# Where the reloads of x and of the last modulation weights are issued, in a conditioned linear-attention and SwiGLU block

## Chip, cores and metric

The kernel runs on one core of one Trainium2 chip. The metric is the device time of one execution in microseconds (us). The engines of a core are named as in the profile: PE (TensorE, matrix products; its weight loads are shown apart as PEld), DVE (VectorE), ACT (ScalarE), POOL (GpSimd) and SP (SyncE, which here issues nearly all DMA transfers).

## What is computed

```python
x = A_x                                            # (1, 2048, 1024), bf16
mod = (silu(c) @ w_mod).reshape(c.shape[0], 6, 1, -1)
sa, ca, ga, sb, cb, gb = (mod[:, i] for i in range(6))

h = layernorm(x) * (1 + ca) + sa
q, k, v = split(h @ wqkv)                          # 32 heads of 32
pq, pk = phi(q), phi(k)                            # phi(t) = (t+1 if t>0 else exp(t)) + 1e-6
kv = einsum('bhsd,bhse->bhde', pk, v)
z = einsum('bhsd->bhd', pk)
o = einsum('bhqd,bhde->bhqe', pq, kv) / (einsum('bhqd,bhd->bhq', pq, z)[..., None] + 1e-6)
x = x + ga * (o @ wo)

h = layernorm(x) * (1 + cb) + sb
x = x + gb * ((silu(h @ w_gate) * (h @ w_up)) @ w_down)     # F = 3584
```

There are 2048 rows of 1024 elements; everything is bf16 in DRAM, and the vector c is a single row.

## The kernel before

The 2048 rows are 16 row tiles of 128 rows (`st` 0 to 15), four of which make a chunk of 512 (`ch` 0 to 3). The kernel is one straight program. Every operation is recorded once through helpers (`P.pe`, `P.dve`, `P.act`, `P.pool`, `P.dma`); each engine runs its operations in the order in which they were recorded, and a recorder derives from the reads and writes of each operation which semaphores it has to wait for. All recorded operations therefore carry the line of one helper, L176, in the profile; a few that are recorded otherwise have their own (L905 for the load of Wo, L955 for `rb`, L1079 for gate and up weights). `P.wait_for(engine, ops)` (L195) puts only a wait into an engine's stream. `P.dma` goes to SP unless another queue is named.

The stages in the order of PE's work:

- *q and k.* The tile `XRES` (16 row tiles of x, 32 KB a partition) is loaded, normalized in place, transposed and scaled, and multiplied with Wq and Wk. After this, `XRES` holds the normalized x and no longer x itself.
- *kv* (`g_group` and `g_evac`, L913 and L920). Sixteen groups `g`, each of 16 matmuls over all row tiles, multiply phi(k) with the normalized x in `XRES`. In the last group, PE reads row tile 0 first and row tile 15 last. Between the groups stand `kvt_mm(half)` (L962), 128 short matmuls with 32 columns that form the 32x32 blocks of kv, and `m_mm(half, nh, banks)` (L972), 16 short matmuls that multiply them with Wo into the tile `MW`; ACT and DVE copy the results of `m_mm` out of PSUM. `scale_pq` (L959) divides phi(q), in `PQT`, by the denominators that stand in `RB`.
- *The Wo stage* (from L1033, in the main from L1083). `wo_part(st, nh, hgs)` (L992) multiplies `PQT` with `MW` for row tile `st` and half `nh` of the columns, eight matmuls of 128x512 into one of four PSUM banks in turn. `wo_res(st, nh)` (L998) is the residual on DVE: it adds the bank to the row tile in `XRES`, which by then has to hold x again, and takes the row's sum with it. The first halves of the products for row tiles 0 and 1 are run earlier, mixed with `kvt_mm(1)` and `m_mm(1, ...)`. The order of the residuals is (0,0), (1,0) in the first turn of the loop, (0,1), (1,1) in the second, and from then on both halves of row tile `st` in turn `st`. Beside it, ACT squares each finished row tile (`ln2_sq`), DVE makes mean and variance after every fourth (`ln2_rstd`), and DVE accumulates `macc(STGX[0], kt)` in turns 1 to 6, eight steps of 1024 columns by which a part of the modulation is formed without PE. Turn 7 normalizes chunk 0 and issues its transposition (`th2_dma`) and the first four pairs of gate and up weights (`gu_load`).
- *The FFN* (from L1107). For each chunk: 28 tiles of F with gate and up products, then the product with W_down, the final residual and the stores. In chunk 0, `macc(STGX[1], ft)` is run for the first eight tiles of F.

The two tiles `STGX[0]` and `STGX[1]` (2 MB each) take parts of `w_mod` and lie where `RB` was; so the load into `STGX[1]` (`stgx2`) may start when `scale_pq` of the last four head groups has read `RB`. The reloads of x write into `XRES` and so wait for the last kv group to have read the row tiles in question: `xr0` to `xr3` one row tile each (256 KB), `xr4`, `xr5` and `xr6` four row tiles each (1 MB, rows 512-1023, 1024-1535 and 1536-2047). The order on SP around the change is: `stgx1` (during group 10), `stgx2`, `xr0` to `xr3`, `xr4` to `xr6`, the transposition of the modulation part (`macc_split`, the tile `mhlt`), `th2_dma`, `gu_load`.

Of the kernel before, what the change touches and what calls it, by code (L numbers as in the profile page):

```python
# [9 lines left out]
ALU = mybir.AluOpType  # L10
# [252 lines left out]
def bass_adaLN_cond__linear_attn_block__swiglu_ffn__prompt_kernel(  # L263
# [16 lines left out]
    NCH = 4  # L280
# [5 lines left out]
    with ExitStack() as es:  # L286
# [6 lines left out]
        def T(name, off, shape, dt):  # L293
            n = 1
            for s_ in shape[1:]:
                n *= s_
            assert off % 32 == 0 and off + n * mybir.dt.size(dt) <= ARENA, (name, off, shape)
            return nc.alloc_sbuf_tensor_at(name, shape, dt, offset=base + off)

        KB = 1024  # L300
        XRES = T("xres", 0, [128, NST, D], BF16)
# [30 lines left out]
        SUMXH = T("sumxh", SM + 2816, [128, NST, 2], FP32)  # L332
# [17 lines left out]
        STGX = [T("stgx%d" % i, (72 + 16 * i) * KB, [128, NDT, D], BF16) for i in range(2)]  # L350
# [28 lines left out]
        PS = nc.alloc_psum_tensor("ps", [128, 8, 512], FP32)  # L379
# [5 lines left out]
        xv = A_x[0].rearrange("(t p) d -> p t d", p=128)  # L385
# [6 lines left out]
        wmv = w_mod.rearrange("(kt p) n -> p kt n", p=128)  # L392
        cv8 = c.rearrange("o (kt p) -> (o kt) p", p=128)

        P = _Prog()
# [223 lines left out]
        for f in s0_:  # L619
# [10 lines left out]
               op0=ALU.mult, op1=ALU.mult)  # L630
# [80 lines left out]
        def macc(src, kt):  # L711
            if kt == 0:
                P.dve("tensor_scalar", out=ACC[:], in0=src[:, kt, :], scalar1=SILUF[:, kt:kt + 1], scalar2=None,
                      op0=ALU.mult)
            else:
                P.dve("scalar_tensor_tensor", out=ACC[:], in0=src[:, kt, :], scalar=SILUF[:, kt:kt + 1], in1=ACC[:],
                      op0=ALU.mult, op1=ALU.add)

        def macc_split():
            P.dve("tensor_copy", out=MHL[:, 0, :], in_=ACC[:])  # L720
            P.dve("tensor_tensor", out=MHL[:, 1, :], in0=ACC[:], in1=MHL[:, 0, :], op=ALU.subtract)
            xbar(MHLT[:], MHL[:].rearrange("p i d -> p (i d)"))

        def mod_red():
            P.dve("tensor_reduce", out=RED[:], in_=MHLT[:].rearrange("d (i m) p -> d m i p", i=2),
                  axis=mybir.AxisListType.XY, op=ALU.add)

        def mod_fin_col(idx, plus_one):
            P.dve("tensor_copy", out=MODTMP[:, 0:8], in_=RED[:])
            if plus_one:  # L730
                P.dve("tensor_scalar", out=MODTMP[:, 0:8], in0=MODTMP[:, 0:8], scalar1=1.0, scalar2=None,
                      op0=ALU.add)
            P.dve("tensor_copy", out=MODCOL[:, idx, :], in_=MODTMP[:, 0:8])
# [186 lines left out]
        def g_evac(g):  # L920
            h, dt = g // NDT, g % NDT
            bank = G_BANKS[1 if g == 14 else g % 5]
            i = g % 2
            P.act("activation", out=GTMP[:, i, :], in_=ZB[:, h * 512:(h + 1) * 512], func=ACT.Copy,
                  scale=MODCOL[:, 1, dt:dt + 1])
            P.dve("scalar_tensor_tensor", out=G[:, dt, h * 512:(h + 1) * 512], in0=PS[:, bank, :],
                  scalar=MODCOL[:, 0, dt:dt + 1], in1=GTMP[:, i, :], op0=ALU.mult, op1=ALU.add)
# [44 lines left out]
        def m_mm(half, nh, banks):  # L972
            for k in range(4):
                for g in range(4):
                    h = (g + k) % 4
                    P.pe("matmul", out=PS[32 * h:32 * h + 32, banks[g], :],
                         lhsT=KVT[32 * g:32 * g + 32, half, 32 * h:32 * h + 32],
                         rhs=WO[32 * g:32 * g + 32, 4 * half + h, nh * 512:(nh + 1) * 512], start=True, stop=True,
                         skip_group_check=True)
            for g in range(4):  # L980
                dst = MW[:, 4 * half + g, nh * 512:(nh + 1) * 512]
                if g % 2 == 0:
                    P.act("activation", out=dst, in_=PS[:, banks[g], :], func=ACT.Copy)
                else:
                    P.dve("tensor_copy", out=dst, in_=PS[:, banks[g], :])
# [6 lines left out]
        def wo_part(st, nh, hgs):  # L992
            bank = WO_BANKS[(2 * st + nh) % 4]
            for hg in hgs:
                P.pe("matmul", out=PS[:, bank, :], lhsT=PQT[:, hg, st * 128:(st + 1) * 128],
                     rhs=MW[:, hg, nh * 512:(nh + 1) * 512], start=(hg == 0), stop=(hg == NHG - 1))

        def wo_res(st, nh):  # L998
            bank = WO_BANKS[(2 * st + nh) % 4]
            xs = XRES[:, st, nh * 512:(nh + 1) * 512]  # L1000
            P.dve("scalar_tensor_tensor", out=xs, in0=PS[:, bank, :], scalar=1.0, in1=xs, op0=ALU.mult,
                  op1=ALU.add, accum_out=SUMXH[:, st, nh:nh + 1])

        ev = 0
        for g in range(16):
# [21 lines left out]
            if g == 10:  # L1027
                P.dma("stgx1", STGX[0][:], wmv[:, :, 3072:4096])
        g_evac(15)
        P.dma("stgx2", STGX[1][:], wmv[:, :, 5120:6144])  # L1030
        for st in range(4):
            P.dma("xr%d" % st, XRES[:, st, :], xv[:, st, :])
        wo_part(0, 0, range(4))  # L1033
# [5 lines left out]
        wo_part(1, 0, range(1, 4))  # L1039
        wo_part(1, 1, range(4))  # L1040
        m_mm(1, 1, [4, 5, 7, 6])
        for ch in range(1, NCH):
            P.dma("xr%d" % (3 + ch), XRES[:, 4 * ch:4 * ch + 4, :], xv[:, 4 * ch:4 * ch + 4, :])

        def ln2_rstd(ch):
            sl = slice(4 * ch, 4 * ch + 4)
# [8 lines left out]
        def ln2_xn(st):  # L1055
            P.dve("tensor_scalar", out=XN2[:, :, st % 4, :], in0=XRES[:, st, :].rearrange("p (dt q) -> p dt q", q=128),
                  scalar1=MEAN2[:, st:st + 1], scalar2=RSTD2[:, st:st + 1], op0=ALU.subtract, op1=ALU.mult)

        def th2_dma():
            xbar(H2T[:].rearrange("p dt (j s) -> p (dt j) s", j=4), XN2[:].rearrange("p dt j q -> p (dt j q)"))  # L1060

        def th2_mod():
            for dt in range(NDT):
                P.pool("tensor_scalar", out=H2T[:, dt, :], in0=H2T[:, dt, :], scalar1=MODCOL[:, 2, dt:dt + 1],
                       scalar2=MODCOL[:, 3, dt:dt + 1], op0=ALU.mult, op1=ALU.add)

        def ln2_sq(st):
            P.act("activation", out=JUNK[:], in_=XRES[:, st, :], func=ACT.Square, accum_out=SUMSQ[:, st:st + 1])
            if st % 4 == 3:
                ln2_rstd(st // 4)  # L1070

        def gu_load(q):
            slot = q % 4
            p = q % 14
            g_out, g_in = GUG[slot][:], wgv[:, :, p * 256:(p + 1) * 256]
            u_out, u_in = GUU[slot][:], wuv[:, :, p * 256:(p + 1) * 256]

            def fn(e):
                return [e.dma_start(out=g_out, in_=g_in), e.dma_start(out=u_out, in_=u_in)]  # L1079

            P.add("sp", fn, reads=[], writes=[g_out, u_out], lane="gu%d" % slot, ninc=2, tag="gu_load")

        for st in range(NST):  # L1083
            for (sw, nh) in (((0, 0), (1, 0)), ((0, 1), (1, 1)))[st] if st < 2 else ((st, 0), (st, 1)):
                wo_part(sw, nh, range(4, 8) if st < 2 else range(8))
                wo_res(sw, nh)
            if st >= 1:
                ln2_sq(st - 1)
            for kt in ((), (0,), (1,), (2, 3), (4,), (5,), (6, 7))[st] if st < 7 else ():
                macc(STGX[0], kt)  # L1090
            if st == 6:
                macc_split()
            if st == 8:
                mod_red()
                mod_fin_col(3, False)
            if st == 7:
                for jj in range(4):
                    ln2_xn(jj)
                th2_dma()
            if st == 8:  # L1100
                th2_mod()
            if st == 7:
                for q in range(4):
                    gu_load(q)
        ln2_sq(NST - 1)
        out_ops = []
        for ch in range(NCH):  # L1107
            nxt = ch + 1 if ch + 1 < NCH else None
            for ft in range(NFT):
# [27 lines left out]
                if nxt is None and ft in (8, 12):  # L1137
# [3 lines left out]
                          in1=GB_B[:, 896:1024].unsqueeze(1).to_broadcast([128, f1 - f0, 128]), op=ALU.mult)  # L1141
# [5 lines left out]
            for j in range(4):  # L1147
                st = 4 * ch + j
# [7 lines left out]
                for nh in range(2):  # L1156
                    i = nh
                    parts = [(0, 384, bb + 1), (384, 512, 4)] if last and nh == 1 else [(0, 512, bb + nh)]
                    for (c0, c1, pb) in parts:
# [5 lines left out]
                        xs = XRES[:, st, nh * 512 + c0:nh * 512 + c1]  # L1165
# [45 lines left out]
```

## Time and profile before

| what | value |
|---|---|
| median of 9 runs | 830.0 us (829.29 to 830.31) |
| profiled execution, its own time | 829.29 us |
| its span in the profile | 827.6 us |
| last kv group's matmuls end, Wo stage's go on | about 186.0 us |
| first gate matmul of the FFN | 244.86 us |
| granted TensorE clock | 1.00 |
| DMA traffic over the whole run | 119.32 MB, mean 144 GB/s |

The span runs from the first to the last instruction that the profiler recorded, and the rest of the execution's time lies around it. Times inside the profile count from the span's start. "Busy" is the time in which an engine executes something; registers, branches, semaphores and the issuing of DMAs don't count. In a timeline row the columns are start, length, engine, line, operation, output tile and input tile, how many instructions were merged, and in brackets the idle time before them and what ended it. In a row of waits they are the waiting engine and tile, who released it, the idle time in total, how often, and the longest. SPq rows are DMA issues, and their length is that of the issuing alone.

### The profile page before, as it was taken

The numbers are of one execution on the slowest core, as the hardware profiler recorded it, in microseconds if no ns is written. First come the engines' busy times: TensorE is split into PE (matmuls) and PEld (weight loads), VectorE is DVE, ScalarE is ACT, GpSimd is POOL, SyncE is SP. The second block draws the span as 40 slices with busy tenths as digits, with TensorE's granted clock in tenths as the row PEclk, the third lists the DMA queues.
The fourth block names the chain that finished last, engine by engine and source line by source line (L and its number), as shares of the span: only waits on it lengthen the run. The fifth ranks groups of instructions, "written<-read, shape, count | busy, mean of one in ns | idle before, by whom it ended". The sixth has DMA issues, their size and how long they took to land.

```text
span 827.6 us, 10508 instructions
## 1 busy us (share of the span) xinstructions
PE 820.8 (99%) x4323; PEld 376.2 (45%) x4323; DVE 311.6 (38%) x664; ACT 197.4 (24%) x336; POOL 40.5 (5%) x59
## 2 busy tenths in 40 slices
PE   8999999999999999999999999999999999999998
PEld 4544444444444444444444444444444444444444
DVE  5797997476945521121221112122111211221111
ACT  4757643123242111011111101111110111111011
POOL 1010000000130000030000003000000300000000
PEclk9999999999999999999999999999999999999999
DMA  9969656866397985700455570045557004553000
GB/s 320 289 151 230 150 160 158 183 183 259 70 260 231 288 255 156 177 27 20 131 152 151 153 178 30 20 127 155 150 152 187 26 17 126 152 152 88 0 26 26
DMA packets 199360, 119.32 MB, mean 144 GB/s; under 512 B 57992, under 2 KB 183056, under 8 KB 199312
## 3 DMA queue, kind: packets, MB, share of 16 engines
q1 hardware_dynamic: 199296, 118.65, 53.1%
q8 instruction: 34, 0.56, 0.3%
q14 instruction: 14, 0.11, 0.0%
q10 hardware_dynamic: 16, 0.00, 0.0%
HBM read 100.67 MB, written 4.33 MB: 127 GB/s over the span
## 4 chain that ended last, share of the span: by engine, by line
PE 99%; DMA 0%; DVE 0%; issue 0%; ACT 0%; SPq 0%
PE ps L176 99%; DMA xres<-in_A_x_dram 0%; DVE stats L176 0%; ACT xres L176 0%; SPq L176 0%; DVE xres L176 0%; DVE mv L176 0%; DVE nmr L176 0%
## 5 line engine op out<-in xcount | busy, mean ns | idle before, releaser
L176 PE MATMUL ps<-h2t,gug 128*128 128x512 bf16 x896 | 211.7, 379 | 0.0
L176 PE MATMUL ps<-h2t,guu 128*128 128x512 bf16 x896 | 211.7, 379 | 0.0
L176 DVE TENSOR_TENSOR at<-sg,ps 128x512 bf16<-128x512 bf16 x112 | 77.0, 687 | 282.8 <-PE ps L176 281.2
L176 ACT ACTIVATE sg<-ps 128x512 bf16<-128x512 f32 x112 | 66.9, 597 | 309.7 <-PE ps L176 309.7
L176 PEld LDWEIGHTS ps<-h2t,guu 128*128 128x128 bf16 x896 | 87.7, 98 | 105.7
L176 PEld LDWEIGHTS ps<-h2t,gug 128*128 128x128 bf16 x896 | 87.6, 98 | 105.5
L176 PE MATMUL ps<-wd_a,at 128*128 128x512 bf16 (+1 forms) x512 | 112.4, 377 | 0.0
L176 PE MATMUL ps<-ht,wqk 128*128 128x512 bf16 x512 | 111.7, 379 | 0.0
L176 PE MATMUL ps<-wd_b,at 128*128 128x512 bf16 (+1 forms) x384 | 85.0, 377 | 0.0
L176 DVE TENSOR_TENSOR ut<-att,gb_b 128x512 bf16<-128x512 bf16 (+1 forms) x32 | 14.7, 458 | 166.5 <-ACT att L176 166.5
L176 PEld LDWEIGHTS ps<-wd_a,at 128*128 128x128 bf16 x512 | 50.1, 98 | 59.7
L176 PEld LDWEIGHTS ps<-ht,wqk 128*128 128x128 bf16 x512 | 49.4, 98 | 58.8 <-DVE ht L176 0.4
L176 ACT ACTIVATE att<-ps 128x512 bf16<-128x512 f32 (+1 forms) x32 | 17.4, 591 | 182.1 <-PE ps L176 182.1
L176 PEld LDWEIGHTS ps<-wd_b,at 128*128 128x128 bf16 x384 | 37.6, 98 | 44.7
L176 PE MATMUL ps<-mw,pqt 128*128 128x512 bf16 x256 | 56.2, 379 | 1.2 <-issue 1.2
L176 PE MATMUL ps<-pk,xres 128*128 128x512 bf16 x256 | 56.2, 379 | 0.0
L176 POOL TENSOR_SCALAR h2t<-h2t,modcol 128x512 bf16<-128x512 bf16 x32 | 26.3, 837 | 383.0 <-DMA h2t<-xn 383.0
L176 ACT ACTIVATE e<-ps 128x512 bf16<-128x512 f32 x56 | 33.1, 603 | 31.7 <-PE ps L176 20.2
L176 PEld LDWEIGHTS ps<-mw,pqt 128*128 128x128 bf16 x256 | 24.7, 98 | 31.5 <-issue 1.9
L176 PEld LDWEIGHTS ps<-pk,xres 128*128 128x128 bf16 x256 | 24.7, 98 | 29.9 <-issue 0.9
L176 ACT ACTIVATE junk<-xres 128x1024 bf16<-128x1024 bf16 x24 | 25.4, 1058 | 35.8 <-DVE xres L176 35.5
L176 DVE SCALAR_TENSOR_TENSOR xres<-ps,xres 128x512 bf16<-128x512 f32 x32 | 21.5, 688 | 13.1 <-PE ps L176 12.9
(107 smaller groups left out, 337.0 us busy)
## 6 DMA issues: line engine op xcount, KB each, us to landing
gug<-in_B_w_gate_dram SPq DMA_DIRECT2D x56, 512.0 KB, 3.9
guu<-in_B_w_up_dram SPq DMA_DIRECT2D x56, 512.0 KB, 5.2
xres<-in_A_x_dram SPq DMA_DIRECT2D x20, 256.0 KB, 7.9
rb<-recip_den SPq DMA_DIRECT2D x8, 512.0 KB, 11.5
stgx<-in_w_mod_dram SPq DMA_DIRECT2D x2, 2048.0 KB, 8.4
wd_a<-in_B_w_down_dram SPq DMA_DIRECT2D x4, 1024.0 KB, 7.3
out_dram<-xres SPq DMA_DIRECT2D x31, 128.0 KB, 1.7
xres<-in_A_x_dram SPq DMA_DIRECT2D x3, 1024.0 KB, 14.1
```

The source lines that it names most:

```text
L176: return getattr(e, method)(**kw)
```

## The change

Two things in the order of SP's program change, and nothing in the order of the other engines.

The load `stgx2` is taken out from before the reloads of x, and `xr4` to `xr6` are taken out from behind the last `m_mm`. All four are issued in the loop of the Wo stage: after turn 0, 1 and 2 SP waits for the last residual recorded in that turn and then issues `xr4`, `xr5` and `xr6`; after turn 3 it waits likewise and issues `stgx2`. The residuals that it waits for are (1,0), (1,1), (2,1) and (3,1). For this, `wo_res` returns the operation that it records. The reloads of row tiles 0 to 3 stay where they were.

```diff
         def wo_res(st, nh):
             bank = WO_BANKS[(2 * st + nh) % 4]
             xs = XRES[:, st, nh * 512:(nh + 1) * 512]
-            P.dve("scalar_tensor_tensor", out=xs, in0=PS[:, bank, :], scalar=1.0, in1=xs, op0=ALU.mult,
-                  op1=ALU.add, accum_out=SUMXH[:, st, nh:nh + 1])
+            return P.dve("scalar_tensor_tensor", out=xs, in0=PS[:, bank, :], scalar=1.0, in1=xs, op0=ALU.mult,
+                         op1=ALU.add, accum_out=SUMXH[:, st, nh:nh + 1])
...
         g_evac(15)
-        P.dma("stgx2", STGX[1][:], wmv[:, :, 5120:6144])
         for st in range(4):
             P.dma("xr%d" % st, XRES[:, st, :], xv[:, st, :])
...
         m_mm(1, 1, [4, 5, 7, 6])
-        for ch in range(1, NCH):
-            P.dma("xr%d" % (3 + ch), XRES[:, 4 * ch:4 * ch + 4, :], xv[:, 4 * ch:4 * ch + 4, :])
...
         for st in range(NST):
             for (sw, nh) in (((0, 0), (1, 0)), ((0, 1), (1, 1)))[st] if st < 2 else ((st, 0), (st, 1)):
                 wo_part(sw, nh, range(4, 8) if st < 2 else range(8))
-                wo_res(sw, nh)
+                done = wo_res(sw, nh)
+            if st < 4:
+                P.wait_for("sp", [done])
+                if st < 3:
+                    ch = st + 1
+                    P.dma("xr%d" % (3 + ch), XRES[:, 4 * ch:4 * ch + 4, :], xv[:, 4 * ch:4 * ch + 4, :])
+                else:
+                    P.dma("stgx2", STGX[1][:], wmv[:, :, 5120:6144])
```

## The prediction

> **What bounds the kernel now.** I read the page's busy times and its chain of waits first, then the waits of PE, then the timelines of PE, SP and DVE around the Wo stage, and last the DMA view cut into narrow windows. The page:
>
> ```profile
> span 827.6 us, 10508 instructions
> PE 820.8 (99%) x4323; PEld 376.2 (45%) x4323; DVE 311.6 (38%) x664; ACT 197.4 (24%) x336; POOL 40.5 (5%) x59
> PE ps L176 99%; DMA xres<-in_A_x_dram 0%; DVE stats L176 0%; ACT xres L176 0%; SPq L176 0%; DVE xres L176 0%; DVE mv L176 0%; DVE nmr L176 0%
> ```
>
> The chain that ended last is PE from end to end, and PE is idle for only 827.6 - 820.8 = 6.8 us. So time can be won only where PE stands idle, and lost only by making it stand. The waits of PE alone, then its timeline across the start of the Wo stage (start, length, tiles, idle time before):
>
> ```profile
> PE ps L176 <- DMA cs<-in_c_dram: 2.2, 1, 2.2
> PE ps L176 <- issue: 1.2, 1, 1.2
> ...
> 187.42 1.20 PE L176 MATMUL ps<-g,wv 128*32 128x32 bf16 x128
> ...
> 191.28 0.43 PE L176 MATMUL ps<-wo,kvt 32*32 32x512 bf16 x16
> 191.65 1.04 PE L176 MATMUL ps<-mw,pqt 128*128 128x512 bf16 x4
> 193.85 2.32 PE L176 MATMUL ps<-mw,pqt 128*128 128x512 bf16 x10 [1.16 <-issue]
> ```
>
> One PE gap of the whole run lies in the stage that the change touches: before 193.85, put down to "issue", which means that no semaphore explains it. The bracket counts from a modelled end. By pace it is a little more: 236 matmuls fill 193.85 to 244.86, 0.216 us each, so after the four that start at 191.65 the next was due at 191.65 + 4 x 0.216 = 192.51, and 193.85 - 192.51 = 1.34 us is lost.
>
> I looked for what "issue" is here. The page counts 34 packets on the queue of kind "instruction" with 0.56 MB, 16.4 KB each: PE's program arriving piece by piece. The DMA view says when one comes. From 187.4 (the start of kvt_mm(1), 128 matmuls in 1.2 us, which uses up instructions far faster than the rest) to 191.4 there is none, and the bulk queue has all 16 engines; then comes one, and PE goes on:
>
> ```profile
> DMA packets 825, 1.56 MB, mean 390 GB/s; under 512 B 63, under 2 KB 63, under 8 KB 825
> q1 hardware_dynamic: 825, 1.56, 105.7%
> ...
> q1 hardware_dynamic: 234, 0.45, 98.9%
> q8 instruction: 1, 0.02, 5.8%
> ```
>
> (The first pair is the window 187.4 to 191.4, the second 191.4 to 192.6.) The twin of this spot is kvt_mm(0) at 166.62: there the traffic ended near 168.9, a packet came in the window 169.2 to 169.4, and PE shows no gap. From the start of the short matmuls to the packet it is 169.3 - 166.6 = 2.7 us there and 191.4 - 187.4 = 4.0 us here, 1.3 us more, which is the size of the gap. My reading: the instruction packet queues behind the reloads. SP's timeline names them:
>
> ```profile
> 169.75 12.59 SPq L176 DMA_DIRECT2D stgx<-in_w_mod_dram x2
> 182.99 6.50 SPq L176 DMA_DIRECT2D xres<-in_A_x_dram x7
> 219.13 1.57 SPq L176 DMA_TRANSPOSE mhlt<-mhl x1
> ```
>
> The second stgx load (2 MB, at 181.9), xr0-3 (1 MB) and xr4-6 (3 MB), 6.3 MB at 390 GB/s, need 16 us, and the slices of DMA are full from 184 to 200, then empty to 220.
>
> **The change, part by part.** *Removed before the stage:* stgx2 and xr4-6. What is left is xr0-3, 1.05 MB issued 182.99 to 184.7, of which the first is held by the last kv group as before. The first bytes of stgx2 moved about 1.4 us after its issue, so xr0-3 move from 184.4 for 1.05 MB / 390 GB/s = 2.7 us and are down by about 187.3, just as kvt_mm(1) begins. The instruction packet then meets empty queues. Its price is not shown for an empty queue at this spot. The nearest row is kvt_mm(0): 2.7 us, packet at 187.4 + 2.7 = 190.1, and with the same distance to resumption (193.85 - 191.44 = 2.4 us) PE could go on at 192.5, when it is due at 192.51: gain 1.34 us at most, 1.3 taken. Bound from the other side: if the packet comes at 4.0 us whatever the traffic, the gain is 0. I take the upper end, because between this packet and the next one (197.6, by the same view, with q1 at 105.2% in between) lie 6 us under full traffic, so delay by traffic is what the rows show.
>
> [...]
>
> Does the 1.3 us arrive at the end? DVE empties the four banks. wo_res(0,0) at 193.04 stands behind the last MW casts and doesn't move; its successors wait for PE (1.25, 0.16, 0.43, 0.96, 0.95 us idle up to 203.54) and follow it. From 204.16 DVE is nearly back to back (7.76 of 8 us in 204 to 212, 7.72 of 8 in 220 to 228), with one idle 0.76 at 213.90 that also waits for PE; PE itself feels DVE only as a weight load 0.4 us late at 227.57. All of this chain starts from a PE event, so it moves as one block; nothing else at a fixed time is in it (stgx1 landed at 169.75 + 8.9 = 178.7). The FFN after it is bound by PE at its pace. Full 1.3 us arrive.
>
> *Added: four waits on SP.* Behind the first stand xr4, xr5, xr6 and stgx2, behind those the mhlt transpose at 219.13. They wait for wo_res(1,0), (1,1), (2,1) and (3,1), which end at 195.7, 197.3, 200.8 and 204.2 in the old times; the issues cost SP about 0.44 us each (its median for xres), so SP is free at about 205, 14 us before mhlt. Cost 0, hidden by SP's idle stretch. DVE, PE and ACT keep their instructions and order.
>
> *Moved: the four landings.* xr4 is first read by wo_res(4,0), at 206.68: 11.0 us after its issue, both in old times, so the lead stays when all shifts. Price of landing: 1 MB on a nearly idle queue took 5.5 us (wd_a at 243.75), the same 1 MB behind the old pile 15.5 us. Its queue will be empty, so I take 5.5; 5.5 us spare. At 15.5 DVE is 4.5 us late, less the 0.76 it has idle: PE loses 3.7. xr5 is needed at 222.07 (24.7 us lead), xr6 at 233.04 (32), stgx2 by its first macc at 249.56 (45, against 8 to 9 us for 2 MB): nothing late even at 15.5. The traffic now runs from about 196 to 212. DVE's residual add takes 0.69 us under traffic at 195 and 0.68 without at 210, ACT's squares 1.06 in both, so overlap costs 0. PE's next instruction packets (197.6 and 217 now) lie about before and after that traffic; 2 x 4323 instructions in 34 packets are 254 each, 127 matmuls with their weight loads, 27 us at the pace here, so a delay of some 5 us is covered. The one packet of the other instruction queue near 210 will now meet stgx2's tail; what it feeds the rows do not say, between 0 and 5 us late, and with engines that run a fraction of PE's instructions I take 0.
>
> **Sum.** The profiled execution took 829.29 us: span 827.6 and 1.7 around it. It is the fastest of the nine runs, 0.7 below their median. 829.29 - 1.3 = 828.0 for an execution like it, 830.0 - 1.3 = 828.7 for the median.
>
> **Rivals.** *The gap is larger in most runs.* The profiled run is the fastest; if the 0.7 us to the median sits in this gap, which depends on how transfers happen to queue, the gain is 1.3 + 0.7 = 2.0: 828.0. For it: the matmul stream itself has a fixed pace, so little else can vary. Against it: the start of the kernel waits for DMA too (cs 2.2 us on PE), and what lies around the span can vary.
> *The gap isn't the traffic's, or merely moves.* Then the packet still comes 4 us after kvt_mm(1), or another one is caught by the new traffic: 830.0. For it: kvt_mm(1) and the 32 m_mm matmuls eat 320 instructions in 4 us, a cause in itself. Against it: kvt_mm(0) does the same without a gap.
> *x rows 512-1023 come late (slower).* One megabyte that must be down 11.0 us after its issue; if it takes over 11.8 (lead plus the 0.76 of DVE), PE stands before row 6 for want of a bank. At 15.5 us: -1.3 + 3.7 = +2.4, 832.4. For it: all three 1 MB reloads took 13 to 15.5 us before. Against it: they queued behind 3 MB and more, and have an empty queue now.
>
> **How the numbers follow.** Forecast 0.60, larger gap 0.17, no gain 0.13, late rows 0.10. Predicted 828.7. Nine runs spread over 1 us, so about 0.2%, 1.66 us, is what can be told from no change; the bounds are 828.34 and 831.66. The forecast's own range is 828.2 to 829.3; 0.08 of its chance lies below 828.34. Faster 0.17 + 0.08 = 0.25; slower 0.07 (the late rows at a price over 1.66); same 0.68. The range goes from 828.0 less 0.3 for the spread of medians, 827.7, to the no-gain case with 0.4, 830.4; it leaves out the late rows and some tails.
>
> **What would show it.** Right: no "issue" wait on PE near 192, an instruction packet near 190, wo_res(1,0) at about 193.7 and the first gate matmul at 243.5; SP issues xr4 near 194.7, stgx2 near 203, xr4 landed in some 5 us; DVE waits nowhere for xres from DMA. Wrong: PE's gap still there or a new one of its size; DVE waiting for "DMA xres" before row 4; a residual add longer than 0.69 us under the moved traffic.

## The result, and the profile after

The changed kernel takes 828.70 us in the median of 16 runs (827.81 to 829.09); the kernel before, run beside it, takes 830.38 us (52 runs, 829.18 to 832.95). The ratio is 0.9975, with a 95% interval of 0.9969 to 0.9981: some 2.1 us, or 1.6 to 2.6; the medians are 1.7 us apart, the means 2.1 (830.62 and 828.55). In a second comparison (below, e7) it was 0.9981, 0.9972 to 0.9989. The forecast was 828.7 us. What its parts are worth is another matter: the first profile shows 1.3 us of gain in the stage, and the rest took experiments to find.

The page of the changed kernel, then its waits of PE alone, then PE's timeline across the start of the Wo stage:

```profile
span 827.0 us, 10507 instructions
PE 821.5 (99%) x4323; PEld 376.4 (46%) x4323; DVE 311.5 (38%) x664; ACT 197.4 (24%) x336; POOL 40.5 (5%) x59
```

```profile
PE ps L176 <- DMA cs<-in_c_dram: 2.2, 1, 2.2
PE ps L176 <- ACT xres L176: 0.8, 1, 0.8
PE ps L176 <- DVE e L176: 0.2, 1, 0.2
```

```profile
186.83 1.46 PE L176 MATMUL ps<-mw,pqt 128*128 128x512 bf16 x6
188.22 1.20 PE L176 MATMUL ps<-g,wv 128*32 128x32 bf16 x128
...
192.08 0.43 PE L176 MATMUL ps<-wo,kvt 32*32 32x512 bf16 x16
192.45 7.73 PE L176 MATMUL ps<-mw,pqt 128*128 128x512 bf16 x35
```

The wait put down to "issue" is gone, and the matmuls go on from 192.45 without a break. The span is only 0.6 us shorter than in the first profile of before, because this execution began later: its Wo stage starts at 186.83 instead of 186.03, a matter of the first loads (DVE waits for a load of x until 6.34 us instead of 5.54). So I compare stages and not spans. From the first Wo matmul to the first gate matmul (244.34 here) the stage takes 244.34 - 186.83 = 57.51 us; before it took 244.86 - 186.03 = 58.83.

The DMA view in two narrow windows, 188.2 to 189.4 and 189.4 to 190.5, shows nearly empty queues behind the start of kvt_mm(1) at 188.22, and then the instruction packet:

```profile
q1 hardware_dynamic: 14, 0.02, 3.8%
...
q8 instruction: 1, 0.02, 5.5%
```

It comes 1.2 us after kvt_mm(1) starts (189.4 - 188.2), against 4.0 us before. The moved loads, by the DMA view around their issues (KB, then us from issue to landing), xr4, xr5, xr6 and stgx2 in this order:

```profile
xres<-in_A_x_dram SPq DMA_DIRECT2D x1, 1024.0 KB, 5.6
...
xres<-in_A_x_dram SPq DMA_DIRECT2D x1, 1024.0 KB, 7.8
...
xres<-in_A_x_dram SPq DMA_DIRECT2D x1, 1024.0 KB, 7.3
...
stgx<-in_w_mod_dram SPq DMA_DIRECT2D x1, 2048.0 KB, 9.6
```

DVE waits nowhere in the stage for a reload, and its residual adds still take 0.68 to 0.69 us each. The first that needs `xr4`, wo_res(4,0), starts 11.0 us after the issue of `xr4` at 195.19, without a wait:

```profile
206.16 0.68 DVE L176 SCALAR_TENSOR_TENSOR xres<-ps,xres 128x512 bf16<-128x512 f32 x1
```

### The profile page after: what moved, and what is told of

Read it like the earlier page. It is cut to its first block, busy times and chain, and to the rows that moved or that the text cites. A ratio compares the mean times of both kernels' runs of the same rounds, so it can differ in the third digit from the quotient of the medians.

```text
span 827.0 us, 10507 instructions
## 1 busy us (share of the span) xinstructions
PE 821.5 (99%) x4323; PEld 376.4 (46%) x4323; DVE 311.5 (38%) x664; ACT 197.4 (24%) x336; POOL 40.5 (5%) x59
## 4 chain that ended last, share of the span: by engine, by line
PE 99%; DMA 1%; DVE 0%; ACT 0%; SPq 0%; issue 0%
PE ps L176 99%; DMA xres<-in_A_x_dram 1%; DVE stats L176 0%; ACT xres L176 0%; SPq L176 0%; DVE xres L176 0%; DVE mv L176 0%; DVE nmr L176 0%
## 5 line engine op out<-in xcount | busy, mean ns | idle before, releaser
L176 PEld LDWEIGHTS ps<-h2t,guu 128*128 128x128 bf16 x896 | 87.7, 98 | 105.7
```

What stands on the lines that cost most here:

```text
L176: return getattr(e, method)(**kw)
```

## The experiments

All times of one group are compared with runs of the kernel before made beside them (830.58 us for e0 to e3, 830.08 for e4 to e7, 831.01 for the last four). "Packet" below is the time from the start of kvt_mm(1) to the instruction packet, "stage" is first Wo matmul to first gate matmul, "kv stage" is first kv matmul to first Wo matmul (59.56 us in the first two profiles).

### Before again (e0)

> The kernel before, unchanged, profiled a second time. Measure: the Wo stage, from its first matmul to the first gate matmul; 58.83 us in the first profile of before, 57.51 after the change (difference 1.32), and 2.07 us by the ratio of the medians. Theory 'the gap varies' : the PE gap behind kvt_mm(1) has another size here, above 1.16 us if the first profile was a lucky one, up to about 2. Rival 'the gap is fixed and the rest of the difference is noise of the start and of the chips': a gap of 1.1 to 1.4 us again, stage 58.7 to 58.9. Ratio to before 1.000.

Measured: ratio 1.000 (0.999 to 1.001), packet 4.0 us, stage 58.78 us. In this profile the gap is the same as in the first, as the rival has it. But there is a second one, of 0.3 us behind kvt_mm(0), and of the 11 times two are far from the others (831.93 and 832.46). One more profile could not say what those two runs had; this was taken up again at the end.

### One half of the change each (e1, e2)

e1 issues stgx2 early again, e2 issues xr4-6 early again; each leaves out the late issue of the same loads (not shown):

```diff
 e1:     g_evac(15)
+        P.dma("stgx2", STGX[1][:], wmv[:, :, 5120:6144])
...
 e2:     m_mm(1, 1, [4, 5, 7, 6])
+        for ch in range(1, NCH):
+            P.dma("xr%d" % (3 + ch), XRES[:, 4 * ch:4 * ch + 4, :], xv[:, 4 * ch:4 * ch + 4, :])
```

> The changed kernel, but stgx2 (2 MB) issued early again, ahead of xr0-3; only xr4-6 issued in the stage. Theory 'the instruction packet waits behind the bulk bytes that are already queued': stgx2 and xr0-3, 3.15 MB from about 183.3 at 390 GB/s, are in the queues until about 191.4, so the packet comes near 191 as before: gap about 1 us or more, stage 58.5 to 58.9, ratio to before about 1.000 (at most 0.5 us faster). Rival 'the 3 MB pile xr4-6 is what delays it': gap gone, stage 57.5, ratio about 0.9975 to 0.9985.

> The kernel before, but stgx2 issued behind the fourth turn of the stage as in the change; xr4-6 stay early. Theory 'behind the bulk bytes already queued': xr0-3 and xr4-6, 4.2 MB from about 184.4, are in the queues until about 195; the packet comes at 191 or later: gap 1 to 2.5 us, stage 58.5 to 60, ratio about 1.000 or slightly above. Rival 'stgx2 alone is to blame because it is ahead of everything': gap gone, stage 57.5, ratio 0.9975 to 0.9985.

PE's timeline, e1 and then e2:

```profile
192.78 1.04 PE L176 MATMUL ps<-mw,pqt 128*128 128x512 bf16 x4
195.20 7.07 PE L176 MATMUL ps<-mw,pqt 128*128 128x512 bf16 x32 [1.38 <-issue]
```

```profile
192.72 1.04 PE L176 MATMUL ps<-mw,pqt 128*128 128x512 bf16 x4
194.85 7.50 PE L176 MATMUL ps<-mw,pqt 128*128 128x512 bf16 x34 [1.09 <-issue]
```

The gap is there in both: packet 4.1 and 3.9 us, stage 59.04 and 58.74 us, ratios 0.9992 (0.9983 to 1.0001) and 0.9994 (0.9986 to 1.0003). Either half of the traffic is enough to delay the packet, and neither half of the edit wins alone what the whole wins. Both rivals, which blamed one of the piles, fall. The bytes asked for ahead of the packet differ (3 MB in e1, 4 MB in e2), and the packet comes at nearly the same time, 4.1 and 3.9 us; so between these two the amount does not set the delay.

### The same transfers, another place in the program (e3)

```diff
         warm(13, bank=3)
+        for _ in range(64):
+            P.pe("matmul", out=PS[:, 3, 0:1], lhsT=IDENT[:], rhs=E1[:, 0, 0:1], start=True, stop=True)
```

> The kernel before with all its DMAs where they were, and 64 matmuls of one column more among the warm-up matmuls at the very start of PE's program (their product is never read); this shifts PE's program by 128 instructions, half a 16 KB packet, so that the packet that came late at 191 is asked for while the queues are empty (near 177) and the next one is not needed until after the traffic. Theory 'PE starves for instructions': gap gone with the same traffic, stage 57.5, time 1.3 to 2 us below before (less at most 0.7 us if the 64 matmuls are not hidden at the start). Rival 'the traffic slows PE in another way, for example its data or its semaphores': gap of 1.2 us remains, stage 58.8, ratio 1.000 or a little above.

PE's timeline, and the DMA view from kvt_mm(1) at 188.8 to 193.5:

```profile
192.67 0.44 PE L176 MATMUL ps<-wo,kvt 32*32 32x512 bf16 x16
193.03 9.24 PE L176 MATMUL ps<-mw,pqt 128*128 128x512 bf16 x42
```

```profile
q1 hardware_dynamic: 967, 1.82, 105.4%
```

The queues are as full as before (105.4% of the 16 engines, against 105.7%) and PE doesn't stop: stage 57.50 us, ratio 0.9981 (0.9972 to 0.9990). A packet came at 180.6, before the traffic, and the next one, late by itself (4.7 us), was not needed yet. This is the cleanest of the runs: the traffic, with the program not starving, cost PE nothing here (57.50 us, against 57.51 in the changed kernel), and the gap is a late piece of PE's own program. It fits that in all eight profiles with the gap (the five of before, e1, e2 and e4) PE stops at the same place of its program, behind the four matmuls that follow the last m_mm. The added matmuls are not hidden at the start: the first transposition of x runs at 9.50 us, against 8.36 to 9.09 in the five profiles of before.

### Shorter rows in the same transfers (e4)

```diff
-        P.dma("stgx2", STGX[1][:], wmv[:, :, 5120:6144])
+        for nh in range(2):
+            P.dma("stgx2%d" % nh, STGX[1][:, :, 512 * nh:512 * nh + 512], wmv[:, :, 5120 + 512 * nh:5632 + 512 * nh])
...
         for st in range(4):
-            P.dma("xr%d" % st, XRES[:, st, :], xv[:, st, :])
+            for nh in range(2):
+                P.dma("xr%d%d" % (st, nh), XRES[:, st, 512 * nh:512 * nh + 512], xv[:, st, 512 * nh:512 * nh + 512])
```

xr4-6 are split in the same way.

> The kernel before with the same bytes at the same places of the order, but stgx2 and all seven reloads of x split in two by columns, so that a contiguous run of a transfer is 1 KB instead of 2 KB (twice the packets, 16 issues on SP instead of 8). Measures: from the start of kvt_mm(1) to the instruction packet, 4.0 us before and 1.2 us after the change; stage 58.8 and 57.5 us. Theory 'a fixed number of packets that the DMA engines have taken in already stands ahead of the instruction packet': half the bytes stand ahead, packet at about 2 to 2.6 us, gap 0 to 0.3, stage 57.5 to 57.8. Rival 'it waits until a given load of bytes is through, or for a share of the memory bandwidth': packet again at about 4 us, gap of 1 us or more, stage 58.5 or more.

The DMA view from kvt_mm(1) at 187.3 to 191.7, which ends with the packet:

```profile
q1 hardware_dynamic: 1603, 1.53, 110.3%
q8 instruction: 1, 0.02, 1.6%
```

Nearly twice the packets and about the same megabytes as before (825 packets, 1.56 MB), and the instruction packet comes no earlier, at 4.4 us; stage 59.41, ratio 1.0010 (1.0001 to 1.0018). My theory of a fixed number of packets ahead of it falls. What remains: full queues add some 3 us to the 1.2 us of a quiet packet, in all the mixes of transfers tried here. Which step of the fetch is slowed, these runs do not show.

### The rows that are needed first, late (e5)

```diff
             if st < 4:
                 P.wait_for("sp", [done])
-                if st < 3:
-                    ch = st + 1
+                if st != 2:
+                    ch = (2, 3, 0, 1)[st]
                     P.dma("xr%d" % (3 + ch), XRES[:, 4 * ch:4 * ch + 4, :], xv[:, 4 * ch:4 * ch + 4, :])
-                else:
+                if st == 3:
                     P.dma("stgx2", STGX[1][:], wmv[:, :, 5120:6144])
```

> The changed kernel with xr5 and xr6 behind the first and second turn, and xr4 (rows 512-1023, the first to be needed) only behind the fourth, with stgx2 behind it: issued near 203.7 instead of 195.2, and wanted by wo_res(4,0) at 206.2. By the price of the forecast (5.5 us to land) xr4 is down near 209, wo_res(4,0) 2.8 us late, DVE catches up by the 0.76 us that it has idle at 213: PE loses about 2 us, stage 59.5, ratio to before about 0.9995 to 1.001 (2 us slower than the changed kernel). Rival 'DVE has more slack than counted, the four banks cover it': stage 57.5 to 58.2. Rival 'the rows come much later': above 60.5.

DVE's timeline at wo_res(4,0), and PE's:

```profile
209.93 0.69 DVE L176 SCALAR_TENSOR_TENSOR xres<-ps,xres 128x512 bf16<-128x512 f32 x1 [3.05 <-DMA xres<-in_A_x_dram]
```

```profile
222.18 7.08 PE L176 MATMUL ps<-mw,pqt 128*128 128x512 bf16 x31 [0.96 <-DVE xres L176]
229.98 16.36 PE L176 MATMUL ps<-mw,pqt 128*128 128x512 bf16 x74 [0.72 <-DVE xres L176]
```

xr4 landed 5.5 us after its issue, DVE stood for 3.05 us, and PE felt it mostly at 222 and 230 (0.15 us earlier, at 210.7), when by my reading the four banks were full. Stage 59.78: 59.78 - 57.51 = 2.27 us lost, where 3.05 - 0.76 = 2.29 was the price. Ratio to before 1.0009 (1.0001 to 1.0018); the median of 831.11 is 2.3 us above that of the changed kernel run beside it (828.79, e7). The slower rival of the forecast has its price right; the change is on the safe side of it, because its xr4 lands in 5.6 of the 11.0 us of lead.

### The change with a shifted program, and the change again (e6, e7)

e6 is the changed kernel with e3's 64 matmuls in the room of four warm-up matmuls (`warm(9, bank=3)`).

> The changed kernel with PE's program shifted by 120 instructions: 64 matmuls of one column more and four of the 13 warm-up matmuls fewer, so that the start is not later. The change took the late packet of the Wo stage away; profiles of the second copy of before and of both halves of the change show a second, smaller gap of 0.3 to 0.85 us behind kvt_mm(0), near 172.7, which the first two profiles did not have and the shifted program had not either. Theory 'that gap is a late instruction packet too and comes in some runs': kv stage (first kv matmul to first Wo matmul) 59.55 us, Wo stage 57.5, median below the changed kernel's by 0.2 to 0.6 us, ratio 0.9965 to 0.9975. Rival 'the second gap has another cause, or fewer warm-up matmuls cost as much': at or above the changed kernel, ratio 0.9975 or more.

> The changed kernel again. First profile: Wo stage 57.51 us, 1.32 below before, while the ratio 0.9975 means 2.07 us. Theory 'the change is worth the 1.3 us of the late packet, and the rest of the first comparison is chance': ratio 0.998 to 0.9988, stage 57.5, kv stage 59.55 or up to 0.85 above. Theory 'before has in some of its runs a larger gap than the profiles caught': ratio 0.9970 to 0.998 again, and the runs of before have a tail above 831.5 that this one lacks.

e7: ratio 0.9981 (0.9972 to 0.9989), packet 1.3 us, stage 57.49, kv stage 59.74; its 11 runs reach from 828.22 to 829.34. It lies on the border of the two theories; of the 35 runs of before beside it two are above 831.5, as the second has it. e6: kv stage 59.55, stage 57.50, both free of gaps as expected, and yet a median of 829.45 and a ratio of 0.9989 (0.9980 to 0.9997). So the rival's bound holds, but where e6 loses is not shown. In its profile PE waits 0.8 us for the first loads of `wca`, yet the first kv matmul comes at 127.60 us, no later than e7's at 127.68. Three of its twelve runs have a granted clock of 0.998, and none of the changed kernel's has. No version beats the changed kernel.

### Catching a long run of before (t1, t2, t3), and the shift without the change (t4)

> The kernel before, one profile, to catch one of its long runs (some 2 in 10 of its times lie above 831.5 us, none of the changed kernel's 27). Theory 'the long runs have a larger gap behind kvt_mm(1)': if this run is above 831.3, its Wo stage is 60 us or more, with the instruction packet later than 5 us after kvt_mm(1) starts; if it is an ordinary one, 58.8 and 4.0. Rival 'the long runs start late': the Wo stage is 58.8 and the first kv matmul comes later than 128.5 us.

> The same as the look before: long run, then Wo stage 60 us or more by the one theory, first kv matmul later than 128.5 us by the other; ordinary run, then 58.8 and about 127.

> The same as the look before: long run, then Wo stage 60 us or more by the one theory, first kv matmul later than 128.5 us by the other; ordinary run, then 58.8 and about 127.

> The kernel before with all its DMAs, PE's program shifted by 120 instructions at the start in the room of four warm-up matmuls. Theory 'only the instruction packets cost time, in the kv stage and in the Wo stage': kv stage 59.55 us, Wo stage 57.5, no run above 831, ratio to before 0.9972 to 0.9988 though every transfer stands where it stood. Rival 'the shift costs at the start what it wins': ratio 0.9988 to 1.000.

The five profiles of before, and the two of the changed kernel:

| profile | its time, us | packet, us | next matmul late by, us | stage, us |
|---|---|---|---|---|
| before, first | 829.29 | 4.0 | 1.3 | 58.83 |
| e0 | 830.05 | 4.0 | 1.3 | 58.78 |
| t2 | 830.00 | 4.0 | 1.3 | 58.78 |
| t3 | 830.90 | 4.4 | 1.8 | 59.33 |
| t1 | 832.32 | 4.6 | 2.1 | 61.29 |
| changed, first | 828.77 | 1.2 | 0 | 57.51 |
| e7 | 829.34 | 1.3 | 0 | 57.49 |

t1 is one of the long runs. PE's timeline, and then the view by stretches (length, busy PE, PEld, DVE, ACT and POOL with their instructions, granted clock of PE, DMA share, GB/s):

```profile
192.22 1.04 PE L176 MATMUL ps<-mw,pqt 128*128 128x512 bf16 x4
195.20 11.13 PE L176 MATMUL ps<-mw,pqt 128*128 128x512 bf16 x43 [1.94 <-issue]
```

```profile
194.00:196.00 2.00, 0.80 (x3) 0.30 (x3) 0.30 (x2) 0.00 (x0) 0.00 (x0) 0.92 1.05 390
196.00:198.00 2.00, 2.00 (x6) 0.73 (x5) 0.70 (x2) 0.00 (x0) 0.00 (x0) 0.50 1.06 389
198.00:200.00 2.00, 2.00 (x8) 0.82 (x7) 1.03 (x3) 0.88 (x1) 0.00 (x0) 0.73 1.05 387
200.00:202.00 2.00, 2.00 (x11) 0.88 (x10) 1.57 (x4) 1.42 (x4) 0.00 (x0) 1.00 0.29 102
```

The packet is later by only 0.6 us than in the ordinary runs, and not beyond 5 us as the theory had it, but right behind the gap PE's clock is granted at one half: six matmuls in the 2 us from 196, eleven from 200. From the three shares below one, (0.08 + 0.50 + 0.27) x 2 us = 1.70 us of full-speed work is lost. With the 2.1 us of the gap that is 3.8 us, and 61.29 - 57.50 = 3.79. t3, with 1.8 us of gap, keeps its clock (mean 1.000); its stage and its packet lie between the two cases that were expected. So the half clock followed a gap of 2.1 us, once. That the gap is the cause is argued from the order of events in one profile.

How often before loses its clock can be read from the mean granted clock of each run. Of the 96 runs of before in e0 and beside the experiments, 11 have 0.998, and they took 831.75 to 833.10 us; the other 85 have 1.000, and two of them are above 831.5. t1's 1.70 us are 0.002 of 830 us, so its loss is the size of theirs. All runs of the changed kernel have 1.000.

t4 leaves every transfer where it was and shifts the program alone. PE's timeline, and the DMA view from kvt_mm(1) at 189.1 to 193.7:

```profile
193.01 0.43 PE L176 MATMUL ps<-wo,kvt 32*32 32x512 bf16 x16
193.37 9.89 PE L176 MATMUL ps<-mw,pqt 128*128 128x512 bf16 x45
```

```profile
q1 hardware_dynamic: 946, 1.78, 105.6%
```

Stage 57.50, kv stage 59.55, twelve runs from 828.36 to 830.29, ratio 0.9979 (0.9969 to 0.9989; medians 829.84 and 831.01). So two edits that share nothing but the packet win about the same, and neither has a run above 831.5. t4 pays something at the start: its first kv matmul comes at 128.21 us, against 126.48 to 127.29 in the profiles of before, and three of its runs, like three of e6's, have a clock of 0.998.

## Why the prediction was right, and where it was not

*The gap is a late instruction packet.* Shown by e3 and t4: the packet's place in the program moves, the traffic stays, the gap goes.

*The reloads delay it.* Shown by the change itself (4.0 to 1.2 us) and by e1 and e2. The other row that the forecast leaned on, the 6 us to the next packet, had no quiet row beside it; after the change the two packets stand 3.6 us apart (189.4 and 193.1), so the direction was right. The delay is 4.0 - 1.2 = 2.8 us. I also had it "queue behind the reloads", and e1, e2 and e4 (4.1, 3.9 and 4.4 us) show no clear dependence on how many bytes or packets stand there. The word queue says more than is known.

*The size of one ordinary gap.* Forecast 1.3 us, measured 58.83 - 57.51 = 1.32 us. The first gate matmul was forecast at 243.5; it came at 244.34 in an execution that was 0.80 us later from the start, so at 243.54. That the block moves as one is right. The row that I took for a packet in a quiet queue was wrong, though: 2.7 us behind kvt_mm(0), measured 1.2. That row was itself under the traffic of `rb` (89.7% of the 16 engines from 166.6 to 169.2). In the other profiles it is 3.2 to 4.1 us (3.3 in the changed kernel's first), and where it is longest PE stands there too:

```profile
172.04 1.04 PE L176 MATMUL ps<-pk,xres 128*128 128x512 bf16 x4
173.75 2.75 PE L176 MATMUL ps<-pk,xres 128*128 128x512 bf16 x12 [0.68 <-issue]
```

(e1's timeline.) This smaller gap belongs to both kernels; the change doesn't touch it, and the forecast didn't see it, because the only profile at hand had none. The result didn't hang on it: by 4.0 - 1.3, anything below about 2.7 us leaves no gap. Nor did it hang on the 1.4 us to the first bytes of stgx2, which the trace puts at 1.05 (181.94 to 182.99).

*The four waits and the moved landings cost nothing.* Right: xr4 landed in 5.6 us (5.5 taken), the others in 7.3 to 9.6, nothing waited, no residual add got longer. e5 bears out the price, lateness less 0.76 us, at one point.

*The sum and its rival.* 830.0 - 1.3 = 828.7 is the measured median, partly by luck: the median of before in the larger sample is 830.38, so it fell by 1.7 us, and the ratios say 2.1 and 1.6. The gap of an ordinary run was sized rightly. e0 and t2, at 830.05 and 830.00 us, have the same gap as the first profile, and the 0.7 us between them and it lie ahead of the Wo stage: their first kv matmul comes at 126.96 and 127.21 us instead of 126.48, and e0's kv stage is 0.3 us longer. So the reason of the rival "the gap is larger in most runs" was wrong, though its 2.0 us is near the ratios. What the forecast left out is that some runs pay more: in the stage, t3 pays 0.5 us and t1 2.5 us more than the first profile, t1 mostly by the clock. So the five profiles of before have a mean stage of 59.40 us, 1.9 above the changed kernel's, and a median of 58.83. The price of the clock was in no step of the forecast. Why the medians differ by 1.7 us and not by 1.3 is not shown in full. The forecast's most likely class was a change of less than 0.2%; the ratio of 0.9975 is just beyond it, 0.9981 just within. The rivals "no gain" and "late rows" are excluded, the latter with e5 as its measure.

What stays open: which step of the instruction fetch the traffic slows; whether the clock of the long runs drops where it drops in t1, the only one profiled (the changed kernel has no time above 831.5 us in 27 runs, which fits); and where e6 and t4 lose what the shift wins.

## What to carry to other kernels

Behind 128 short matmuls in 1.2 us PE ran out of its program when the next packet came 4.0 us after their start, and did not when it came after 1.2 us; so here it paid to move bulk transfers that were not needed soon away from that stretch. The sign was an "issue" wait of PE with the DMA engines at 105.7%, and shifting the program by half a packet, with the traffic left alone, told it from a cause that lies in the traffic only (stage 57.50 us in e3 against 58.83). Issue reloads as late as their landing allows (here 5.6 us of landing in 11 us of lead), and measure what lateness costs by making one late (in e5 a wait of 3.05 us on DVE cost 2.27). Take a small gap's price from several profiles: 1.3 us of gap cost 1.32 us here, and 2.1 us of gap were followed by 1.70 us lost to the clock (t1).

## What the runs showed of the hardware

The instruction packet, 16.4 KB in the mean of 34, came 1.2 us after the short matmuls began with the DMA at 14 GB/s (the changed kernel; 1.3 us in e7), and 3.9 to 4.7 us after with full queues (390 GB/s in the first profile of before, 393 in e1 and t1, 388 in e3 and 352 in e4), with packets of about 2 KB and of 1 KB (e4) in them and whether 3 MB (e1) or 6 MB (before) were asked for. PE's clock was granted at 0.50 from 196 to 198 us and at 0.73 from 198 to 200, after a gap of 2.1 us (t1); after one of 1.8 us its mean was 1.000 (t3).
